# Tau-attention with a gated FFN on one core: softmax tiles turned by 64x64 products on quarters of TensorE instead of 128x128 transposes

## The chip, the core and the metric

The kernel runs on one core of one Trainium2 chip. The metric is the device time of one execution in microseconds (us). The kernel before took 859.01 us, the median of three runs (858.6 to 860.33).

## What is computed

For 8 batches, 8 heads, 576 positions and a head size of 64 the reference computes a softmax that keeps only scores within `tau` of the row's maximum, and then a feed-forward block with a convolution of three taps and a gate:

```python
scores = scale * np.matmul(q, k.transpose(0, 1, 3, 2))
thresh = np.max(scores, axis=-1, keepdims=True) - tau
scores = np.where(scores >= thresh, scores, -1000000000.0)
attn = np.exp(scores - np.max(scores, axis=-1, keepdims=True))
attn = attn / (np.sum(attn, axis=-1, keepdims=True) + 1e-09)
x = np.matmul(attn, v)          # heads side by side: 8 x 576 x 512
h = np.maximum(x @ w_in, 0.0)   # 512 -> 1024
...                             # conv_out: three taps of conv_w along the positions
gate = 1.0 / (1.0 + np.exp(-conv_out))
out = (h * gate @ w_out)        # 1024 -> 512
```

All data are float32.

## The kernel before

**Units.** Two heads make a pair, and 128 queries of a pair (or, for the last 64 queries, of two pairs) make a unit: 144 units, 18 to a batch. The function `unit` computes for each of the two heads the scores of 128 queries against 576 keys: four products of 64 by 64 weights and 288 columns, each on its own quarter of the array (line 569). VectorE takes the row maxima (line 581), ScalarE the exponential (line 588), VectorE masks and sums (line 591), and GpSimd or another engine divides by the sum (lines 627 and 629). The result is the tile `em`, with queries on the partitions.

**Turning.** The product with the values needs keys on the partitions, so `em` is turned. 70 of the 144 units go by DMA (`cross`, lines 645 to 671). The other 74 go through TensorE (`transposes`, line 673): nine blocks of 128x128, in three groups of three (`BLOCKS = 3`). A group takes one of two buffers `ps_t` of one PSUM bank, is filled by three transposes with a 128x128 identity (line 684), and ScalarE copies it to the tile `eT` (line 694; line 700 for units of two pairs). All 18 units of batch 0 are turned by TensorE.

**Attention output.** When both pairs of a half of a chunk are turned, `attend` (line 707) multiplies with the values: nine steps, each of four quarter products of 256 or 320 columns (line 720), into the same two `ps_t` buffers, one for each pair. ScalarE and VectorE read them out (lines 728 and 731).

**FFN.** A batch has two chunks of 256 and 320 positions. `mm1` (line 750) and `mm2` (line 801) are full-array products of float32r parts, three for each term; they are the largest part of TensorE's work.

**Order.** Nothing is scheduled by hand. Each step is an entry (`op`) with an engine, a cost, its inputs, its PSUM or SBUF buffers, and a rank lowered by `AHEAD`. `Plan.run` walks through these entries with its own table of costs and writes the instructions of each engine in the order that comes out; on the chip each engine then runs its list in order. For TensorE each entry has a kind: `rows` for quarter products, `turn` for transposes, `full` for the full array, and a table `SWITCH` charges a change of kind. The table charges next to nothing between `turn` and `full`.

The diff touches `transposes`, `attend`, the pool `ps_t` (line 301) and the tables of numbers at the top.

Of the kernel before, what the change touches and what calls it, by code (L numbers as in the profile page):

```python
# [10 lines left out]
F32 = mybir.dt.float32  # L11
# [5 lines left out]
AF = mybir.ActivationFunctionType  # L17
ALU = mybir.AluOpType
PSUM = bass.MemoryType.PSUM

LEAST = 2.0 ** -80
FEW = 4
AHEAD = {'mask': 5.447, 'norm': 7.929, 'parts': -2.68, 'gate': 1.222, 'evac': -0.535, 'low': 0.609, 's': 8.622, 's4': 8.87, 't': 3.177, 'a': 3.675, 'prep': 4.965, 'w': 1.618, 'load': 0.216, 'first': 3.806}

LATENCY = {'pe': 205.37, 'act': 213.173, 'dve': 118.588, 'pool': 62.545, 'ring': 1882.404}

HOLD = {'pool': 134.468, 'dve': 107.493}

NORM = (('pool', 'pool', 'pool', 'pool', 'pool', 'dve'), ('pool', 'pool', 'pool', 'act'))

# [1 line left out]
PIECES = 12  # L32
LOW = ('pool', 'pool')
HPB = 3
MOE = (3, 2)
BACKLOG = {'pool': 3000.0, 'dve': 3000.0, 'act': 9000000000.0}
WRATE = (1.713, 2.547)
ALT = 10.85

FIRST = [(0, 1), (2, 3, 4)]  # L40
GROUPS = [(0, 1), (2, 3, 4)]

EARLY = 0


SWITCH = {
# [3 lines left out]

JOINT = 0

BLOCKS = 3

FAR = 4
VB = 4
# [5 lines left out]
PTB = 1  # L62
QB = 2
CROSS = ((1, 1, 1, 1), (1, 1, 1, 1), (1, 1))
LATE = {'load': 1319.0, 'copy': 4674.0, 'rows': 335.0, 'turn': -88.0}

KEEP = {'rows': 3.322, 'cols': 0.012, 'turn': 0.252, 'full': 0.371}


class Buf:  # L70
# [17 lines left out]
class Plan:  # L88
# [13 lines left out]
    def op(self, engine, ns, fn, w=(), r=(), ahead=0.0, other=None, kind=None, late=0.0, port=False, ring=0.0):  # L102

        i = len(self.ops)
        before = set()
        for x in r:
            before.update(self.wrote[x])
            self.read.setdefault(x, set()).add(i)  # L110
        for x in w:
            before.update(self.wrote.get(x, ()))
            before.update(self.read.pop(x, ()))
            self.wrote[x] = (i,)
        before.discard(i)
# [139 lines left out]
def tile_tau_attention_gated_ffn(  # L255
# [13 lines left out]
    nc = tc.nc  # L269
    P = 128  # L270
    B, NP, _, _, S = qd.shape
    D = 64
# [11 lines left out]
    for b in range(B):  # L284
        for tiles in FIRST if not b else GROUPS:
# [4 lines left out]
                b=b, tiles=tiles, new=(o, end - o), cols=(a0, end - a0), tokens=(k0, (end if end == S else end - 1) - k0),  # L290
# [7 lines left out]
    sm = ctx.enter_context(tc.tile_pool(name="sm", bufs=4))  # L298
    far = ctx.enter_context(tc.tile_pool(name="far", bufs=FAR, space=bass.MemoryType.DRAM))
    ps_s = ctx.enter_context(tc.tile_pool(name="ps_s", bufs=2, space=PSUM))  # L300
    ps_t = ctx.enter_context(tc.tile_pool(name="ps_t", bufs=2, space=PSUM))
    ps_w = ctx.enter_context(tc.tile_pool(name="ps_w", bufs=2, space=PSUM))
    plan = Plan()
    op = plan.op
# [4 lines left out]
    ident = const("ident", [P, P], F32)  # L309
# [8 lines left out]
    for x in fews:  # L318
# [3 lines left out]
            w=[(x, "tau")], r=[(x, 0), (tau_sb, 0)], ahead=8.0  # L322
# [9 lines left out]
    gate = const("gate", [P, 1], F32)  # L332
# [32 lines left out]
    def split(src, n, name, high, low, hr, lr, lead="load"):  # L365
# [16 lines left out]
        lo, hi, a = (stage, 0), (stage, 1), (value, 0)  # L382
        w = AHEAD["w"]

# [99 lines left out]
    ring = [const(f"g{i}", [P, NFB, RING], F32R) for i in "hl"]  # L484
# [188 lines left out]
    def transposes(u, em, dsts):  # L673

        def group(b0, n):

            pt = plan.buf(ps_t, "ps_t", 2, [P, 512], F32, f"ps_t_{u}_{b0}")

            def turns():
                for i in range(n):
                    block = em[:, (b0 + i) * P:(b0 + i + 1) * P]
                    nc.tensor.transpose(out=pt[:, i * P:(i + 1) * P], in_=block, identity=ident[:])  # L684

            op("pe", n * P * 0.852, turns, w=[(pt, 0)], r=[(em, 0), (em, 1), (ident, 0)], ahead=AHEAD["t"], kind="turn")

            def source():
                return pt[:, :n * P].rearrange("p (b g n) -> p g b n", b=n, g=2)

            if dsts[0][0] is dsts[1][0]:
                (eT, g), _ = dsts
                op(
                    "act", act(n * P, True), lambda: nc.scalar.activation(eT[:, g:g + 2, b0:b0 + n, :], source(), AF.Copy),  # L694
                    w=[(eT, (g, b0))], r=[(pt, 0)], ahead=AHEAD["t"] + AHEAD["evac"]
                )
            else:
                for j, (eT, g) in enumerate(dsts):
                    op(
                        "act", act(n * D, True), lambda j=j, eT=eT, g=g: nc.scalar.activation(eT[:, g, b0:b0 + n, :], source()[:, j], AF.Copy),  # L700
                        w=[(eT, (g, b0))], r=[(pt, 0)], ahead=AHEAD["t"] + AHEAD["evac"]
                    )

        for b0 in range(0, NBLK, BLOCKS):
            group(b0, min(BLOCKS, NBLK - b0))

    def attend(of, w, parts):

        pas = [plan.buf(ps_t, "ps_t", 2, [P, 512], F32, f"pa_{i}") for i, *_ in of]
        a = AHEAD["a"]  # L710
        read = parts + [(y[3], 0) for y in of]

        for step in range(NBLK):
            def mm(step=step):
                for (_, p, eT, vt, *_), pa in zip(of, pas):
                    for h in range(2):
                        j, on = h ^ p % 2, slice(h * D, (h + 1) * D)
                        nc.tensor.matmul(  # L720
                            pa[j * D:(j + 1) * D, :w], lhsT=vt[on, step, :], rhs=eT[on, :w // D, step, :],
                            start=(step == 0), stop=(step == NBLK - 1)
                        )

            op("pe", w * 4 / 2.4 + 6, mm, w=[(pa, 0) for pa in pas], r=read, ahead=a, kind="rows")
        for (i, p, eT, vt, x, off), pa in zip(of, pas):
            def high(pa=pa, x=x, off=off):
                nc.scalar.activation(x[:, 0, off:off + w], pa[:, :w], AF.Copy)

            def low(pa=pa, x=x, off=off):  # L730
                nc.vector.tensor_tensor(x[:, 1, off:off + w], pa[:, :w], x[:, 0, off:off + w].bitcast(F32), op=ALU.subtract)

            op("act", act(w, True), high, w=[(x, 0)], r=[(pa, 0)], ahead=a + AHEAD["low"])
            op("dve", dve(w), low, w=[(x, 1)], r=[(pa, 0), (x, 0)], ahead=a + AHEAD["low"])


    def mm1(c, f, xs):
# [118 lines left out]
    for now in range(len(units) + 1):  # L856
        plan.rank = float(now)
        if now < len(units):
            i, t, n = units[now]
            c, p = pairs[i]  # L860
            (o, w), (a0, an) = chunks[c].new, chunks[c].cols
            at = TILES[t][0] - o
# [16 lines left out]
            em = unit(now, sides, n is None)  # L879
# [8 lines left out]
            if ends or alone and units[now + 1][0] != i:  # L888
                waiting = []
                for x in [i // 2 * 2, i // 2 * 2 + 1] if not alone else [i]:  # L890
# [3 lines left out]
                    off = o - a0  # L894
                    if off:
# [3 lines left out]
                            w=[(y, 2)], r=[(z, 0), (z, 1)]  # L899
# [66 lines left out]
```

## Time and profile before

| | |
|---|---|
| time, median of three runs | 859.01 us |
| time of the profiled execution | 857.31 us |
| its span, first to last instruction | 855.2 us |
| TensorE busy | 830.0 us (97%) |
| VectorE, ScalarE, GpSimd busy | 84%, 77%, 48% |
| transposes (line 684) | 666, busy 102.5 us |
| granted TensorE clock | 1.0 throughout |

The trace shows a float32 product as two products and two weight loads, so a group of four quarter products of line 569 is eight records of `PE` and eight of `PEld`. A transpose and a product of line 750 or 801 is one of each. Products are pipelined: their records overlap, and the distance from one start to the next tells the price.

### The profile page before, as it was taken

How to read it: one execution, taken by the hardware profiler on the slowest of the kernel's cores; microseconds unless marked ns; L12 is line 12 of the kernel's file. 1: busy time of each engine (PE TensorE's matmuls, PEld its weight loads, DVE VectorE, ACT ScalarE, POOL GpSimd, SP SyncE). 2: the span in 40 equal slices, each digit the busy share in tenths (PEclk: the TensorE clock that was granted, in tenths of full speed). 3: DMA queues.
4: the chain of work that ended last, by engine and by line, in shares of the span. 5: the costliest groups of instructions: out<-in, count | busy, mean ns of one | idle time of the engine just before them, and what ended most of it. 6: DMA issues, size and time to landing. Idle time of an engine off the chain costs nothing.

```text
span 855.2 us, 20928 instructions
## 1 busy us (share of the span) xinstructions
PE 830.0 (97%) x7710; PEld 609.3 (71%) x7710; DVE 719.6 (84%) x1869; ACT 656.7 (77%) x1300; POOL 410.9 (48%) x549
## 2 busy tenths in 40 slices
PE   6888999999999999999999999999999999999998
PEld 2545667767777677867778677876778677776896
DVE  6999889989979699987979879996979879997542
ACT  5999888877879678887868778886878768886542
POOL 3556544644536345553536535473545535564321
PEclk9999999999999999999999999999999999999999
DMA  7555246679666777578655676688664687555300
GB/s 260 164 164 161 75 110 185 176 206 206 164 149 179 199 196 186 134 217 234 164 149 142 204 195 164 144 211 230 162 180 127 176 215 185 139 135 143 90 26 37
DMA packets 213381, 140.72 MB, mean 165 GB/s; under 512 B 170400, under 2 KB 189088, under 8 KB 213280
## 3 DMA queue, kind: packets, MB, share of 16 engines
q1 hardware_dynamic: 212848, 139.09, 60.9%
q8 instruction: 61, 1.00, 0.5%
q10 hardware_dynamic: 432, 0.30, 0.1%
q14 instruction: 40, 0.33, 0.1%
HBM read 47.34 MB, written 50.72 MB: 115 GB/s over the span
## 4 chain that ended last, share of the span: by engine, by line
PE 86%; ACT 7%; DVE 4%; DMA 1%; issue 1%; POOL 0%; SPq 0%; DVEq 0%; ACTq 0%
PE ph L750 24%; PE po L801 23%; PE ps_s L569 17%; PE pa L720 15%; PE ps_t L684 8%; ACT em L588 2%; ACT eT L694 1%; DVE em L591 1%; DVE few L581 1%; DMA stage<-in_w_in_dram 1%; ACT stage_f L389 1%; PE pw_stage L415 0%; ACT stage L393 0%; ACT em L627 0%; DMA q<-in_qd_dram 0%
## 5 line engine op out<-in xcount | busy, mean ns | idle before, releaser
L629 POOL TENSOR_SCALAR em<-em,few 128x576 f32<-128x576 f32 x217 | 172.8, 804 | 199.1 <-DVE few L615 175.6
L581 DVE TENSOR_REDUCE few<-ps_s 128x1 f32<-128x576 f32 x288 | 209.3, 748 | 62.5 <-PE ps_s L569 60.2
L588 ACT ACTIVATE em<-ps_s,few 128x576 f32<-128x576 f32 x288 | 207.6, 745 | 56.9 <-DVE few L581 56.1
L750 PE MATMUL ph<-x,w1h 128*128 128x322 f32 (+1 forms) x1024 | 237.3, 308 | 0.0
L591 DVE SCALAR_TENSOR_TENSOR em<-ps_s,few,em 128x576 f32<-128x576 f32 x288 | 224.8, 812 | 12.9 <-ACT em L588 5.6
L344 POOL TENSOR_TENSOR gl<-t,gh 128x255 fp32r<-128x255 f32 (+9 forms) x192 | 122.9, 648 | 176.7 <-ACT gh L780 170.8
L750 PEld LDWEIGHTS ph<-x,w1h 128*128 128x128 f32 x1024 | 172.7, 189 | 20.7 <-issue 13.4
L569 PE MATMUL ps_s<-k,q 64*64 64x288 f32 x2048 | 164.4, 423 | 10.9 <-DVE em L591 5.5
L720 PE MATMUL pa<-eT,v 64*64 64x256 f32 (+1 forms) x2304 | 153.8, 404 | 0.0
L750 PE MATMUL ph<-x,w1l 128*128 128x322 f32 (+1 forms) x512 | 151.3, 295 | 0.0
L720 PEld LDWEIGHTS pa<-eT,v 64*64 64x64 f32 x2304 | 91.4, 133 | 49.2 <-issue 1.5
L801 PE MATMUL po<-w2h,gh 128*128 128x512 f32 x288 | 119.8, 416 | 0.0
L694 ACT ACTIVATE eT<-ps_t 128x384 f32<-128x384 f32 x216 | 102.3, 505 | 19.7 <-PE ps_t L684 18.8
L569 PEld LDWEIGHTS ps_s<-k,q 64*64 64x64 f32 x2048 | 67.0, 134 | 68.0 <-issue 24.7
L801 PE MATMUL po<-w2h,gl 128*128 128x512 f32 x288 | 112.9, 392 | 0.0
L801 PE MATMUL po<-w2l,gh 128*128 128x512 f32 x288 | 112.7, 391 | 0.0
L684 PE MATMUL ps_t<-ident,em 128*128 128x128 f32 x666 | 102.5, 280 | 8.8 <-ACT eT L694 5.6
L684 PEld LDWEIGHTS ps_t<-ident,em 128*128 128x128 f32 x666 | 76.0, 141 | 42.9 <-ACT eT L694 14.7
L765 DVE SCALAR_TENSOR_TENSOR t<-hp,cr 128x321 f32<-128x321 f32 (+1 forms) x128 | 78.5, 614 | 22.2 <-ACT hp L759 21.3
L750 PEld LDWEIGHTS ph<-x,w1l 128*128 128x128 f32 x512 | 96.8, 189 | 0.2
L339 POOL COPY parts<-em 128x1152 uint16<-128x1152 uint16 x70 | 82.6, 1180 | 17.2 <-POOL em L629 4.8
L772 ACT ACTIVATE t<-t,cm 128x321 f32<-128x321 f32 (+1 forms) x128 | 68.6, 538 | 27.3 <-DVE t L765 21.1
(73 smaller groups left out, 936.6 us busy)
## 6 DMA issues: line engine op xcount, KB each, us to landing
rows<-parts SPq DMA_DIRECT2D x70, 576.0 KB, 3.5
q<-in_qd_dram SPq DMA_DIRECT2D x63, 256.0 KB, 3.3
v<-in_vc_dram SPq DMA_DIRECT2D x36, 288.0 KB, 4.2
out_dram<-ot SPq DMA_DIRECT2D x36, 256.0 KB, 2.9
k<-in_kp_dram SPq DMA_DIRECT2D x31, 288.0 KB, 3.8
stage<-in_w_in_dram SPq DMA_DIRECT2D x8, 512.0 KB, 4.8
stage<-in_w_out_dram SPq DMA_DIRECT2D x8, 512.0 KB, 3.9
eT<-rows SPq DMA_TRANSPOSE x140, 4.2
```

The costliest lines, as they stand in the source:

```text
L339: engines[e].tensor_copy(dst, src)
L344: engines[e].tensor_tensor(dst, x, y, op=ALU.subtract)
L569: nc.tensor.matmul(ps[g * D:(g + 1) * D, AT + c * CH:AT + (c + 1) * CH], lhsT=q(on, h), rhs=k[on, h * CH:(h + 1) * CH], start=True, stop=True)
L581: nc.vector.tensor_reduce(few[:, nm], scores(), op=ALU.max, axis=mybir.AxisListType.XY, negate=True)
L588: nc.scalar.activation(view(), scores(), AF.Exp, bias=few[:, nm])
L591: nc.vector.scalar_tensor_tensor(view(), scores(), few[:, th], view(), op0=ALU.is_ge, op1=ALU.mult, accum_out=few[:, total])
L629: engines[e].tensor_scalar(sl, sl, LEAST, few[:, 10 + h:11 + h], op0=ALU.add, op1=ALU.mult)
L684: nc.tensor.transpose(out=pt[:, i * P:(i + 1) * P], in_=block, identity=ident[:])
L694: "act", act(n * P, True), lambda: nc.scalar.activation(eT[:, g:g + 2, b0:b0 + n, :], source(), AF.Copy),
L720: nc.tensor.matmul(pa[j * D:(j + 1) * D, :w], lhsT=vt[on, step, :], rhs=eT[on, :w // D, step, :], start=(step == 0), stop=(step == NBLK - 1))
L750: nc.tensor.matmul(ph[:, :an], lhsT=w1[w][:, cb, fs], rhs=xs[cb][:, h, :an], start=(cb == 0 and i == 0), stop=(cb == NCB - 1 and i == 2))
L801: nc.tensor.matmul(po[:], lhsT=x[:, f, at:at + P], rhs=w[:, f, :], start=(f == 0 and i == 0), stop=(f == NFB - 1 and i == 2))
```

## The change

In `transposes` a block of 128x128 is no longer turned in one transpose. Four plain float32 products, each with a 64x64 part of `em` as weights and a 64x64 part of the identity as the moving operand, turn it on the four quarters of the array. The rows of the upper and the lower half go to separate PSUM banks, so a buffer has two banks, and there is one buffer where there were two of one bank. A bank holds five blocks at most (`BLOCKS = 5`), so nine blocks go in groups of five and four, and ScalarE reads out 148 times for the 74 units in place of 222 groups. `attend` takes the same buffer, with a bank for each pair, as one piece. Turning now has the kind `rows`.

All the tables that set the order have other values (a line of them is shown), `MOE` swaps how `mm1` and `mm2` alternate, and `EARLY = 1` puts the `mm2` work of the first chunk ahead by one chunk.

```diff
-AHEAD = {'mask': 5.447, 'norm': 7.929, ... 't': 3.177, 'a': 3.675, ...}
+AHEAD = {'mask': 0.536, 'norm': 8.333, ... 't': 4.212, 'a': 3.072, ...}
-MOE = (3, 2)
+MOE = (2, 3)
-EARLY = 0
+EARLY = 1
-BLOCKS = 3
+BLOCKS = 5
+TURN = 110.0
-    ps_t = ctx.enter_context(tc.tile_pool(name="ps_t", bufs=2, space=PSUM))
+    ps_t = ctx.enter_context(tc.tile_pool(name="ps_t", bufs=1, space=PSUM))
...
-            pt = plan.buf(ps_t, "ps_t", 2, [P, 512], F32, f"ps_t_{u}_{b0}")
+            pt = plan.buf(ps_t, "ps_t", 1, [P, 2, 512], F32, f"ps_t_{u}_{b0}")
             def turns():
                 for i in range(n):
-                    block = em[:, (b0 + i) * P:(b0 + i + 1) * P]
-                    nc.tensor.transpose(out=pt[:, i * P:(i + 1) * P], in_=block, identity=ident[:])
-            op("pe", n * P * 0.852, turns, w=[(pt, 0)], r=[(em, 0), (em, 1), (ident, 0)], ahead=AHEAD["t"], kind="turn")
+                    for g in range(2):
+                        on = slice(g * D, (g + 1) * D)
+                        for j in range(2):
+                            at = (b0 + i) * P + j * D
+                            nc.tensor.matmul(
+                                pt[j * D:(j + 1) * D, g, i * D:(i + 1) * D], lhsT=em[on, at:at + D], rhs=ident[on, on],
+                                start=True, stop=True
+                            )
+            op("pe", n * TURN + 10, turns, w=[(pt, 0)], r=[(em, 0), (em, 1), (ident, 0)], ahead=AHEAD["t"], kind="rows")
             def source():
-                return pt[:, :n * P].rearrange("p (b g n) -> p g b n", b=n, g=2)
+                return pt[:, :, :n * D].rearrange("p g (b n) -> p g b n", n=D)
...
-        pas = [plan.buf(ps_t, "ps_t", 2, [P, 512], F32, f"pa_{i}") for i, *_ in of]
+        pt = plan.buf(ps_t, "ps_t", 1, [P, 2, 512], F32, f"pa_{of[0][0]}")
+        pas = [(lambda on, n=n: pt[on, n, :w]) for n in range(len(of))]
```

Two places show how the order moves. The first is TensorE in the seventh batch, where unit 122 is turned (`ps_t_122`; `po` is `mm2`, `ph` is `mm1`, `ps_s` are scores, and the number after the name of a unit's group is its first block). Before:

```order
L684 MATMUL ps_t_122_0_8974<-ident_99,em_122_8786 128x128 x3
L801 MATMUL po_26_8960<-w2h_766,gh_1146 128x512
L801 MATMUL po_26_8960<-w2h_766,gl_1181 128x512
L801 MATMUL po_26_8960<-w2l_813,gh_1146 128x512
L684 MATMUL ps_t_122_3_8988<-ident_99,em_122_8786 128x128 x3
L684 MATMUL ps_t_122_6_8992<-ident_99,em_122_8786 128x128 x3
```

And now:

```order
L810 MATMUL po_26_10551<-w2l_1047,gh_1469 128x512
L689 MATMUL ps_t_122_0_10599<-ident_99,em_122_10335 64x64 x20
L571 MATMUL ps_s_127_0_10624<-k_56_9009,q_56_10327 64x288 x4
L571 MATMUL ps_s_127_1_10631<-k_56_9009,q_56_10327 64x288 x4
L759 MATMUL ph_12_0_10639<-x_48_9803,w1h_298 128x256
L759 MATMUL ph_12_0_10639<-x_48_9803,w1l_367 128x256
L759 MATMUL ph_12_0_10639<-x_48_9803,w1h_298 128x256
L689 MATMUL ps_t_122_5_10646<-ident_99,em_122_10335 64x64 x16
L759 MATMUL ph_12_0_10639<-x_49_9808,w1h_298 128x256
```

Before, the groups of unit 122 stand between full-array products and touch no quarter product. Now each group is itself quarter work: the first shares its visit with the scores of unit 127, the second stands alone between products of `mm1`.

The second place is ScalarE, where unit 65 is read out (`eT<-ps_t`; `em<-ps_s` is the exponential, `gh` and `t` belong to the gate, `parts` to the turning by DMA). Before:

```order
L694 ACTIVATE eT_29_4796<-ps_t_65_0_4786 128x2x192
L588 ACTIVATE em_67_4804<-ps_s_67_0_4765,few3_87 128x9x64
L588 ACTIVATE em_67_4804<-ps_s_67_1_4779,few3_87 128x9x64
L780 ACTIVATE gh_1146<-t_5_5_4724 128x129
L780 ACTIVATE gh_1146<-t_5_5_4724 128x192
L337 ACTIVATE parts_66_4819<-em_66_4711 128x1152
L772 ACTIVATE t_5_6_4775<-t_5_6_4775,cm_577 128x321
L694 ACTIVATE eT_29_4796<-ps_t_65_3_4791 128x2x192
L694 ACTIVATE eT_29_4796<-ps_t_65_6_4807 128x2x192
```

And now:

```order
L702 ACTIVATE eT_29_5727<-ps_t_65_0_5802 128x2x320
L629 ACTIVATE em_67_5692<-em_67_5692,few3_87 128x9x64
L590 ACTIVATE em_68_5832<-ps_s_68_1_5794,few0_77 128x9x64
L781 ACTIVATE t_5_7_5837<-t_5_7_5837,cm_642 128x321
L339 ACTIVATE parts_67_5851<-em_67_5692 128x1152
L789 ACTIVATE gh_1469<-t_5_7_5837 128x129
L789 ACTIVATE gh_1469<-t_5_7_5837 128x192
L590 ACTIVATE em_69_5903<-ps_s_69_0_5864,few1_83 128x9x64
L702 ACTIVATE eT_29_5727<-ps_t_65_5_5882 128x2x256
```

Three readings of 384 elements a partition have become two of 640 and 512.

More of the change, by code (lines that the diff above doesn't have):

```diff
@@ L22 @@
 FEW = 4
-AHEAD = {'mask': 5.447, 'norm': 7.929, 'parts': -2.68, 'gate': 1.222, 'evac': -0.535, 'low': 0.609, 's': 8.622, 's4': 8.87, 't': 3.177, 'a': 3.675, 'prep': 4.965, 'w': 1.618, 'load': 0.216, 'first': 3.806}
-LATENCY = {'pe': 205.37, 'act': 213.173, 'dve': 118.588, 'pool': 62.545, 'ring': 1882.404}
-HOLD = {'pool': 134.468, 'dve': 107.493}
+AHEAD = {'mask': 0.536, 'norm': 8.333, 'parts': -2.514, 'gate': 1.343, 'evac': 1.378, 'low': 0.932, 's': 8.729, 's4': 8.608, 't': 4.212, 'a': 3.072, 'prep': 4.235, 'w': 2.203, 'load': 0.26, 'first': 4.822}
+LATENCY = {'pe': 189.128, 'act': 211.145, 'dve': 120.916, 'pool': 41.891, 'ring': 1550.868}
+HOLD = {'pool': 133.953, 'dve': 45.87}
 NORM = (('pool', 'pool', 'pool', 'pool', 'pool', 'dve'), ('pool', 'pool', 'pool', 'act'))
@@ L34 @@
 HPB = 3
-MOE = (3, 2)
-BACKLOG = {'pool': 3000.0, 'dve': 3000.0, 'act': 9000000000.0}
+MOE = (2, 3)
+BACKLOG = {'pool': 6860.0, 'dve': 3000.0, 'act': 9000000000.0}
 WRATE = (1.713, 2.547)
-ALT = 10.85
+ALT = 7.12
 FIRST = [(0, 1), (2, 3, 4)]
 GROUPS = [(0, 1), (2, 3, 4)]
-EARLY = 0
+EARLY = 1
 SWITCH = {
@@ L64 @@
 CROSS = ((1, 1, 1, 1), (1, 1, 1, 1), (1, 1))
-LATE = {'load': 1319.0, 'copy': 4674.0, 'rows': 335.0, 'turn': -88.0}
-KEEP = {'rows': 3.322, 'cols': 0.012, 'turn': 0.252, 'full': 0.371}
+LATE = {'load': 1775.0, 'copy': 6300.0, 'rows': 792.0, 'turn': -471.0}
+KEEP = {'rows': 3.245, 'cols': 0.008, 'turn': 0.262, 'full': 0.112}
 class Buf:
@@ L720, in mm @@
                         nc.tensor.matmul(
-                            pa[j * D:(j + 1) * D, :w], lhsT=vt[on, step, :], rhs=eT[on, :w // D, step, :],
+                            pa(slice(j * D, (j + 1) * D)), lhsT=vt[on, step, :], rhs=eT[on, :w // D, step, :],
                             start=(step == 0), stop=(step == NBLK - 1)
                         )
-            op("pe", w * 4 / 2.4 + 6, mm, w=[(pa, 0) for pa in pas], r=read, ahead=a, kind="rows")
+            op("pe", w * 4 / 2.4 + 6, mm, w=[(pt, 0)], r=read, ahead=a, kind="rows")
         for (i, p, eT, vt, x, off), pa in zip(of, pas):
             def high(pa=pa, x=x, off=off):
-                nc.scalar.activation(x[:, 0, off:off + w], pa[:, :w], AF.Copy)
+                nc.scalar.activation(x[:, 0, off:off + w], pa(slice(0, P)), AF.Copy)
             def low(pa=pa, x=x, off=off):
-                nc.vector.tensor_tensor(x[:, 1, off:off + w], pa[:, :w], x[:, 0, off:off + w].bitcast(F32), op=ALU.subtract)
-            op("act", act(w, True), high, w=[(x, 0)], r=[(pa, 0)], ahead=a + AHEAD["low"])
-            op("dve", dve(w), low, w=[(x, 1)], r=[(pa, 0), (x, 0)], ahead=a + AHEAD["low"])
+                nc.vector.tensor_tensor(x[:, 1, off:off + w], pa(slice(0, P)), x[:, 0, off:off + w].bitcast(F32), op=ALU.subtract)
+            op("act", act(w, True), high, w=[(x, 0)], r=[(pt, 0)], ahead=a + AHEAD["low"])
+            op("dve", dve(w), low, w=[(x, 1)], r=[(pt, 0), (x, 0)], ahead=a + AHEAD["low"])
     def mm1(c, f, xs):
```

## The prediction

> **What bounds the kernel now.** I read the page's head and its chain first, then the engines by stretches of the span, then TensorE's waits.
>
> ```profile
> span 855.2 us, 20928 instructions
> PE 830.0 (97%) x7710; PEld 609.3 (71%) x7710; DVE 719.6 (84%) x1869; ACT 656.7 (77%) x1300; POOL 410.9 (48%) x549
> PE 86%; ACT 7%; DVE 4%; DMA 1%; issue 1%; POOL 0%; SPq 0%; DVEq 0%; ACTq 0%
> ```
>
> TensorE is busy for 97% of the span and carries 86% of the chain that ended last. The stretches show that this isn't one regime but two (columns: the stretch, its length, then busy time of PE, PEld, DVE, ACT and POOL):
>
> ```profile
> 0.00:20.00 20.00, 11.48 (x83) 5.36 (x83) 13.16 (x37) 11.32 (x21) 5.69 (x22) 1.00 0.75 254
> 20.00:80.00 60.00, 50.62 (x466) 28.90 (x462) 56.62 (x158) 57.63 (x114) 32.71 (x38) 1.00 0.56 179
> 80.00:100.00 20.00, 19.02 (x202) 14.39 (x202) 17.56 (x41) 17.72 (x42) 14.21 (x13) 1.00 0.26 77
> 100.00:300.00 200.00, 198.99 (x1886) 144.28 (x1879) 175.71 (x455) 159.95 (x314) 96.93 (x130) 1.00 0.68 170
> 300.00:500.00 200.00, 199.86 (x1916) 148.82 (x1915) 173.23 (x460) 157.01 (x308) 97.69 (x130) 1.00 0.68 182
> 500.00:700.00 200.00, 199.35 (x1905) 147.63 (x1898) 173.92 (x457) 154.42 (x301) 97.68 (x131) 1.00 0.68 179
> 700.00:800.00 100.00, 99.11 (x950) 75.94 (x951) 86.72 (x227) 76.83 (x155) 50.42 (x67) 1.00 0.60 158
> ```
>
> From 100 to 800 us TensorE is idle for only 2.7 us of 700 (1.01 + 0.14 + 0.65 + 0.89). There, whatever TensorE gets to do beyond today's work lengthens the kernel one for one, and whatever the other engines save is worth nothing. In the first 100 us TensorE is idle for 18.9 us; from 20 to 80 us ScalarE is busy 57.63 us of 60 and VectorE 56.62, so this opening is theirs. The waits of TensorE after 100 us agree (engine, line, whom it waited for: us in total, times, longest):
>
> ```profile
> PE ps_s L569 <- DVE em L591: 2.1, 3, 0.9
> PE ps_t L684 <- ACT eT L694: 0.3, 1, 0.3
> ```
>
> So the question is what the change adds to or takes from TensorE's own stream: the price of a block, and the price of changing between quarters and the full array.
>
> **What a change of mode costs.** A stretch of the timeline near 416 us has every kind of change (start, length, engine, line, tile, count):
>
> ```profile
> 415.80 0.28 PE L750 MATMUL ph<-x,w1l 128*128 128x256 f32 x1
> 415.92 0.28 PE L750 MATMUL ph<-x,w1h 128*128 128x256 f32 x1
> 416.04 0.82 PE L684 MATMUL ps_t<-ident,em 128*128 128x128 f32 x6
> 416.61 0.36 PE L750 MATMUL ph<-x,w1h 128*128 128x256 f32 x1
> 416.81 0.28 PE L750 MATMUL ph<-x,w1l 128*128 128x256 f32 x1
> ...
> 418.19 0.28 PE L750 MATMUL ph<-x,w1l 128*128 128x256 f32 x1
> 418.31 0.28 PE L750 MATMUL ph<-x,w1h 128*128 128x256 f32 x1
> 418.51 1.20 PE L569 MATMUL ps_s<-k,q 64*64 64x288 f32 x16
> 419.65 0.87 PE L684 MATMUL ps_t<-ident,em 128*128 128x128 f32 x6
> ```
>
> A full-array product of 256 columns starts 0.12 us after the one before it. The first transpose follows at the same 0.12, and the way back is free as well: six transposes last 0.82 us, the last alone 0.27 (the median of the row below), so it began at 416.59; the second full product behind it starts at 416.81, 0.22 later, which is one transpose (0.11) and one product (0.12). Transposes among full products cost no change.
>
> ```profile
> L684 PE MATMUL ps_t<-ident,em x666: 269/273/476, 12.3 to 793.8; 128*128 128x128 f32 x167
> 428.73 1.15 PE L569 MATMUL ps_s<-k,q 64*64 64x288 f32 x16
> 419.29 0.42 PE L569 MATMUL ps_s<-k,q 64*64 64x288 f32 x4
> 402.00 0.72 PE L569 MATMUL ps_s<-k,q 64*64 64x288 f32 x8
> 402.65 0.39 PE L750 MATMUL ph<-x,w1h 128*128 128x256 f32 x1
> 402.87 0.28 PE L750 MATMUL ph<-x,w1l 128*128 128x256 f32 x1
> 402.99 0.40 PE L750 MATMUL ph<-x,w1h 128*128 128x256 f32 x2
> ```
>
> Into the quarters: scores start 0.20 after the last full product instead of 0.12, and sixteen of them last 1.20 us behind a full product against 1.15 behind other quarter products (at 428.73), because the first weight load isn't hidden. That is 0.08 to 0.09 and 0.05: 0.14 us. Out of them to the full array: four quarters run side by side as one set, a set alone lasts 0.42, and in a run of four sets the next starts (1.15 - 0.42)/3 = 0.243 us later. The second set of the eight at 402.00 began at 402.72 - 0.42 = 402.30, so a third would have come at 402.54; the full product came at 402.65, 0.11 late, and the one after it took 0.22 instead of 0.12. Together 0.21 us. Out to a transpose: the last set began at 419.29, the next was due at 419.53, the transpose came at 419.65, and six of them took 0.87 instead of 0.82: 0.16 us.
>
> **How often.** Counting in TensorE's order of instructions: before, it leaves the quarters 87 times for a full product and 49 times for a transpose, and enters them 135 times (31 of these from a transpose, which no row here prices apart; I take 0.14 too). After, it leaves them 150 times, always for a full product, and enters them 149 times. Leaving: 150 x 0.21 - 87 x 0.21 - 49 x 0.16 = 31.5 - 18.3 - 7.8 = +5.4 us. Entering: 14 x 0.14 = +2.0 us. Up to the scores of batch 1 it leaves them 18 times against 21 before, so the surplus lies wholly in the steady part. Changes that were free, transposes next to full products, are what paid for nothing before; their absence saves nothing.
>
> **What a block costs.** Before: (0.82 - 0.273)/5 = 0.109 us for a transpose. After, a block is two sets of four quarter products of 64 columns. No such product is in the trace. The nearest rows are the scores, 0.243 us for 288 columns, and the products with the values:
>
> ```profile
> 425.27 3.63 PE L720 MATMUL pa<-eT,v 64*64 64x256 f32 x64
> 428.51 0.40 PE L720 MATMUL pa<-eT,v 64*64 64x256 f32 x4
> 419.05 0.15 PEld L569 LDWEIGHTS ps_s<-k,q 64*64 64x64 f32 x4
> ```
>
> Sixteen sets in 3.63 us, less the last one's 0.40, are 0.215 us for 256 columns. Both give 0.84 ns a column, so 64 columns give 0.054 us a set and 0.108 a block. The weights of the next set are loaded meanwhile; a load that isn't hidden showed as 0.05, so load and stream are about equally long and neither should hold up the other much. I take 0.111: 666 x 0.002 = +1.3 us. The lower bound is 0.108 (-0.7 us), for a column takes no less in any row. The upper one is the spacing per product that a long run shows: 3.63/64 = 0.057 us, eight to a block, 0.45 us, or +229 us; below the rivals say why it isn't my value.
>
> Products of different quarters do start closer than that: four of them, each 0.402 long at the least (row below), are over in 0.42 us at 419.29, so they start within 0.02 us, and four weight loads lie within 0.15.
>
> ```profile
> L569 PE MATMUL ps_s<-k,q x2048: 402/403/740, 4.1 to 779.4; 64*64 64x288 f32 x187
> ```
>  The Trainium skill, "TensorE: Matmul & The Clock Gate" (Wait — 56ns, not 53.3ns?), says that the distance between starts never falls below about 25 ns, however few columns a product has. By that, eight products would make a block of at least 0.20 us and the sum about +61 us instead of +1.3. The four starts within 0.02 us speak against it for products of different quarters, in short bursts; no row shows them kept up.
>
> **ScalarE and the single buffer.** Reading out has these neighbours:
>
> ```profile
> L694 ACT ACTIVATE eT<-ps_t 128x384 f32<-128x384 f32 x216 | 102.3, 505 | 19.7 <-PE ps_t L684 18.8 <-ACT t L772 0.7
> L808 ACT ACTIVATE ot<-po 128x512 f32<-128x512 f32 x36 | 21.3, 596 | 31.7 <-PE po L801 31.4
> L728 ACT ACTIVATE x<-pa 128x320 fp32r<-128x320 f32 x32 | 12.1, 433 | 7.0 <-PE pa L720 6.9
> 416.56 0.49 ACT L694 ACTIVATE eT<-ps_t 128x384 f32<-128x384 f32 x1 [0.45 <-PE ps_t L684]
> ```
>
> From 320 to 512 elements it takes 0.163 us more, 0.85 ns each, so 640 cost about 0.70 us. A unit takes 0.60 + 0.70 = 1.30 us against 3 x 0.505 = 1.52: 0.2 us saved, 15 us over 74 units, of which the steady part keeps nothing. In the opening ScalarE is full; 14 units are turned before the scores of batch 1, so at most 3 us. I take -2 us, bounds 0 and -3.
>
> The second group of a unit must now wait until the first is read out. ScalarE began 0.52 us after the first of three transposes at 416.04, so 0.30 after the last; with 0.70 of reading and a hand-back of some 0.05 that is 1.05 us from the last start. In the order, 30 of the 116 groups that follow a group have no more between them than two scores' sets (four sets, 0.97 us), and lack up to 0.1 us each; the others have more. I take +1 us; bounds 0, and 10 if ScalarE comes 0.3 late at each of those 30. Behind a late group wait the scores and FFN products in TensorE's list, and so VectorE's maxima. `attend` held both buffers before as well, and its read-out has at least 2 us of other products behind it: nothing. The `mm2` work of chunk 0 that `EARLY` moves is the same work and lies in mid-kernel, covered by TensorE's own full list; at the end the list still closes with the last chunk. Nothing, and DMA on SP has the same 354 issues in both orders.
>
> **Sum.** 5.4 + 2.0 + 1.3 + 1.0 - 2.0 = +7.7 us on the profiled execution of 857.3 us (span 855.2): 865.0. The median of the runs, 859.0, lies 1.7 above that execution, so I expect 866.7 us. A measurement of this kernel can tell about 0.2%, 1.7 us, from no change.
>
> **Rivals.**
> - *The opening gives it back (not slower).* 14.8 us of TensorE's 18.9 idle us in the first 100 lie after its first product at about 4.1 us (those before it can't be had), and 2.7 us later on. Without my -2, the sum is 868.7; if the new order and ScalarE's relief win back half to all of the 17.5 us, the time is 851 to 860. It decides from 9.7 us: there the kernel is back at 859. For it: ScalarE is the fullest engine there and is what the change relieves. Against it: the relief is 3 us, VectorE has the same 56.62 of 60 us to do, and less than the full amount is only a draw. I give 0.18, of which 0.13 faster and 0.05 within 0.2%.
> - *A block costs about twice as much.* If load and stream of a quarter don't overlap when both are 0.05 us, a block is 2 x (0.054 + 0.05) = 0.21 us: 666 x 0.10 = +67 us, 932 us; if starts are what holds, it sets in where a product takes more than 0.111/8 = 0.014 us to issue, and by the long run's 0.057 it would be 1094 us. For it: 16 instructions in 0.11 us is denser than any long run here, where 64 products took 3.63 us. Against it: those bursts, and the loads that start with the set before them. 0.08.
> - *The one buffer makes TensorE wait.* ScalarE is 78% busy in order (157.01 of 200 us); if it came 0.1 us late at each of 148 groups, that would be 15 us in place of 1: 881 us. For it: no second buffer takes up a delay any more. Against it: before, the same hand-over cost 0.3 us after the opening. 0.08.
>
> The forecast itself gets 0.66 (862 to 874 us), of which 0.03 ends within 0.2%. So faster 0.13, the same 0.08, slower 0.79. The range 857 to 882 us leaves out the twofold block and the better part of the first rival, and takes in the third and both ends of the read-out term.
>
> **What would show it.** In the new profile, twenty turning products (40 records) in a row should take 0.56 us from the first start to the next product's, at 64 columns; transposes' 666 records give way to 5328 of the new form. The first product behind the quarters should still come 0.11 late and take 0.10 more, 150 times. TensorE's idle time after 100 us should stay below 5 us, and the opening should end some 2 us sooner at most. I am wrong if a block takes under 0.105 or over 0.13 us, if the first 100 us hold more than 6 us more of TensorE's work, or if waits for the read-out exceed 5 us.

## The result and the profile after

| | before | after |
|---|---|---|
| median | 859.03 us (4 runs, 858.6 to 860.33) | 868.94 us (4 runs, 868.16 to 870.91) |
| profiled execution, its span | 857.31, 855.2 us | 870.91, 869.1 us |
| mean granted TensorE clock in it | 1.0 | 0.996 |

The changed kernel takes 1.0125 times as long (95% interval 1.0109 to 1.0141): 9.9 us more by the medians. The profiled execution of after is the slowest of its four, the profiled one of before lay below its median, so the two traces stand 13.9 us apart by their spans; some 4 us of that lie between single executions and medians, and the text comes back to them. The head of the page and its chain:

```profile
span 869.1 us, 30149 instructions
PE 844.7 (97%) x12372; PEld 639.9 (74%) x12372; DVE 725.8 (84%) x1869; ACT 656.4 (76%) x1223; POOL 417.0 (48%) x550
PE 88%; ACT 5%; DVE 4%; issue 1%; DMA 1%; SPq 1%; POOL 0%; ACTq 0%; DVEq 0%
```

TensorE carries 88% of the chain and is 14.7 us busier; VectorE is 6.2 us busier with the same 1869 instructions, ScalarE's busy time is what it was. By stretches (stretch, length, busy time of PE, PEld, DVE, ACT, POOL, then the granted clock):

```profile
0.00:20.00 20.00, 11.23 (x209) 7.20 (x209) 13.19 (x38) 11.39 (x19) 5.74 (x21) 1.00 0.77 244
20.00:80.00 60.00, 51.62 (x1005) 27.96 (x1001) 52.07 (x145) 53.37 (x97) 30.59 (x35) 0.94 0.52 171
80.00:100.00 20.00, 18.88 (x319) 13.93 (x319) 18.38 (x44) 18.26 (x36) 14.01 (x13) 1.00 0.20 61
100.00:300.00 200.00, 198.59 (x3065) 148.03 (x3055) 177.63 (x461) 157.34 (x290) 101.04 (x132) 1.00 0.70 170
300.00:500.00 200.00, 199.43 (x2902) 154.17 (x2901) 173.70 (x452) 155.89 (x287) 98.81 (x130) 1.00 0.73 178
500.00:700.00 200.00, 199.88 (x2908) 156.59 (x2910) 175.30 (x457) 154.62 (x286) 99.63 (x131) 1.00 0.72 177
700.00:800.00 100.00, 99.64 (x1448) 75.78 (x1437) 89.01 (x227) 75.50 (x141) 49.13 (x65) 1.00 0.62 159
```

From 100 to 800 us TensorE is again idle for only 2.5 us (1.41 + 0.57 + 0.12 + 0.36), as little as before. There the extra time is work and changes of mode, not waiting; TensorE's waits of that part say the same (engine, line, whom it waited for: us in total, times, longest):

```profile
PE pa L729 <- ACT eT L708: 0.8, 1, 0.8
PE ps_t L689 <- ACT eT L702: 0.5, 1, 0.5
PE ph L759 <- ACT hp L768: 0.4, 1, 0.4
```

TensorE waits 0.5 us for the single buffer here. In the opening ScalarE and VectorE have less to do (53.37 and 52.07 us from 20 to 80 us, where before had 57.63 and 56.62), and the granted clock stands at 0.94, where before had 1.00. Two short stretches hold all of the lost clock:

```profile
43.40:46.80 3.40, 2.98 (x52) 1.76 (x55) 2.56 (x8) 1.78 (x4) 1.45 (x2) 0.50 0.00 0
74.10:77.50 3.40, 3.40 (x24) 1.22 (x20) 2.60 (x6) 2.63 (x5) 1.38 (x2) 0.50 0.05 16
```

**The new product.** Two turning groups in the timeline (start, length, engine, line, tile, count), the first alone between full products, the second ahead of scores:

```profile
226.28 0.28 PE L759 MATMUL ph<-x,w1l 128*128 128x256 f32 x1
226.39 0.28 PE L759 MATMUL ph<-x,w1h 128*128 128x256 f32 x1
226.60 0.81 PE L689 MATMUL ps_t<-ident,em 64*64 64x64 f32 x40
227.34 0.50 PE L810 MATMUL po<-w2h,gh 128*128 128x512 f32 x1
227.68 0.39 PE L810 MATMUL po<-w2h,gl 128*128 128x512 f32 x1
227.91 0.39 PE L810 MATMUL po<-w2l,gh 128*128 128x512 f32 x1
...
306.71 0.69 PE L689 MATMUL ps_t<-ident,em 64*64 64x64 f32 x32
307.23 0.67 PE L571 MATMUL ps_s<-k,q 64*64 64x288 f32 x8
```

And the row of the tile (shortest, median, longest):

```profile
L689 PE MATMUL ps_t<-ident,em x5328: 213/218/366, 11.5 to 812.2; 64*64 64x64 f32 x198
```

Eight sets of four behind a full product take 307.23 - 306.71 = 0.52 to the next quarter product; less the 0.05 for the first weight load that isn't hidden, 0.47/8 = 0.059 us a set. The ten sets at 226.60 agree: 0.81, less the last set's 0.24 (0.218 and the 0.02 within a set) and 0.05, over nine steps is 0.058. Over eight inner steps of each group of ten in the trace, the median of a step is 0.0584. A block of two sets thus costs 0.117 us, not 0.111.

The changes of mode cost what they cost before. The turning starts 0.21 after a product that is otherwise followed at 0.12 (0.09, and 0.05 for the load); the full product comes at 227.34, 0.74 after the first start, where 0.05 + 10 x 0.0584 = 0.63 are the sets: 0.11 late, and the one behind it takes 0.34 instead of 0.23: 0.22 in all.

The readings of ScalarE (elements, count, busy time and mean ns):

```profile
L702 ACT ACTIVATE eT<-ps_t 128x640 f32<-128x640 f32 x72 | 50.6, 702 | 7.5 <-PE ps_t L689 7.4
L702 ACT ACTIVATE eT<-ps_t 128x512 f32<-128x512 f32 x72 | 43.1, 599 | 23.4 <-PE ps_t L689 22.8
```

They take 0.702 and 0.599 us, to the hundredth what was estimated.

**The bill.** TensorE's order, priced with distances from start to start, splits the span from the first score to the last product. "Work" is every product at its distance (a transpose 0.109, a turning block 0.117); "changes" are the changes of mode in the order at the mean distances of these traces (0.216 out to a full product, 0.167 out to a transpose, 0.142 in); "rest" is what is left: waiting, and time at half clock. The opening runs from the first score to the first score of unit 36, the first of batch 2.

| us | opening: work, changes, rest | later: work, changes, rest | sum |
|---|---|---|---|
| before | 147.4, 14.3, 25.2 | 619.5, 32.4, 8.2 | 847.0 |
| after | 147.0, 14.3, 29.6 | 625.1, 39.2, 5.6 | 860.8 |

The whole order has 6.9 us more of changes of mode (before rounding), 5.2 us more of work (666 x 0.0078), and 1.8 us more of rest: 4.4 more in the opening, 2.6 less later. (2.0 us of the later work is `mm2` that stood ahead of unit 36 before.)

### The profile page after: what moved, and what is told of

It is laid out like the page before. It is cut to its first block, busy times and chain, and to the rows that moved or that the text cites. A ratio compares the mean times of both kernels' runs of the same rounds, so it can differ in the third digit from the quotient of the medians.

```text
span 869.1 us, 30149 instructions
## 1 busy us (share of the span) xinstructions
PE 844.7 (97%) x12372; PEld 639.9 (74%) x12372; DVE 725.8 (84%) x1869; ACT 656.4 (76%) x1223; POOL 417.0 (48%) x550
## 4 chain that ended last, share of the span: by engine, by line
PE 88%; ACT 5%; DVE 4%; issue 1%; DMA 1%; SPq 1%; POOL 0%; ACTq 0%; DVEq 0%
PE ph L759 23%; PE po L810 23%; PE ps_s L571 16%; PE pa L729 16%; PE ps_t L689 9%; DVE em L593 1%; ACT em L590 1%; ACT eT L702 1%; DVE few L583 1%; DMA rows<-parts 1%; PE pw_stage L417 1%; SPq L671 1%; DVE t L774 0%; ACT stage_f L391 0%; ACT em L629 0%
## 5 line engine op out<-in xcount | busy, mean ns | idle before, releaser
L631 POOL TENSOR_SCALAR em<-em,few 128x576 f32<-128x576 f32 x218 | 175.5, 812 | 200.4 <-DVE few L617 145.1
L590 ACT ACTIVATE em<-ps_s,few 128x576 f32<-128x576 f32 x288 | 206.7, 741 | 51.7 <-DVE few L583 49.4
L759 PE MATMUL ph<-x,w1h 128*128 128x322 f32 (+1 forms) x1024 | 229.0, 304 | 0.4 <-ACT hp L768 0.4
L346 POOL TENSOR_TENSOR gl<-t,gh 128x255 fp32r<-128x255 f32 (+9 forms) x192 | 125.9, 666 | 169.3 <-ACT gh L789 165.0
L759 PEld LDWEIGHTS ph<-x,w1h 128*128 128x128 f32 x1024 | 170.1, 189 | 20.2 <-issue 8.6
L689 PEld LDWEIGHTS ps_t<-ident,em 64*64 64x64 f32 x5328 | 100.1, 136 | 47.6 <-ACT eT L702 15.6
L729 PEld LDWEIGHTS pa<-eT,v 64*64 64x64 f32 x2304 | 96.0, 133 | 46.7 <-ACT eT L702 1.9
L689 PE MATMUL ps_t<-ident,em 64*64 64x64 f32 x5328 | 111.0, 223 | 9.8 <-ACT eT L702 7.0
L702 ACT ACTIVATE eT<-ps_t 128x640 f32<-128x640 f32 (+1 forms) x144 | 93.7, 650 | 30.9 <-PE ps_t L689 30.2
L339 ACT ACTIVATE parts<-em 128x1152 uint16<-128x1152 uint16 x70 | 81.6, 1166 | 7.7 <-POOL em L631 5.7
```

Of the source, the lines that this page charges most:

```text
L346: engines[e].tensor_tensor(dst, x, y, op=ALU.subtract)
L590: nc.scalar.activation(view(), scores(), AF.Exp, bias=few[:, nm])
L631: engines[e].tensor_scalar(sl, sl, LEAST, few[:, 10 + h:11 + h], op0=ALU.add, op1=ALU.mult)
L689: nc.tensor.matmul(pt[j * D:(j + 1) * D, g, i * D:(i + 1) * D], lhsT=em[on, at:at + D], rhs=ident[on, on], start=True, stop=True)
L729: nc.tensor.matmul(pa(slice(j * D, (j + 1) * D)), lhsT=vt[on, step, :], rhs=eT[on, :w // D, step, :], start=(step == 0), stop=(step == NBL ...
L759: nc.tensor.matmul(ph[:, :an], lhsT=w1[w][:, cb, fs], rhs=xs[cb][:, h, :an], start=(cb == 0 and i == 0), stop=(cb == NCB - 1 and i == 2))
```

## The experiments

"Before" was timed again with them: medians 858.71 (with the first four), 858.65 (with the next four) and 857.89 us (with the last three).

**The same order with transposes.** After's order, groups and buffer, but each block is one transpose:

```diff
-                    for g in range(2):
...
+                    nc.tensor.transpose(out=pt[:, i // 4, i % 4 * P:(i % 4 + 1) * P], in_=block, identity=ident[:])
```

> The changed kernel with its order, its groups of five and four and its single buffer untouched, instruction for instruction, but each block is turned by one 128x128 transpose again. Theory (changes of mode and the price of a block): counted in this order, it leaves the quarters 63 times to a full product (0.216 us) and 81 times to a transpose (0.167), enters them 143 times (0.142 to 0.145), and passes 150 times between transposes and full products for nothing; that is 48.0 us of changes against 53.6, and 666 blocks cost 0.109 instead of the 0.117 that the new profile shows, 5.2 us less. Together 10.8 us less than the changed kernel: 858 us. Rival one (the new order is at fault, whatever turns the blocks): it stays at 868 to 869 us. Rival two (the single buffer makes TensorE wait): it stays above 865 us, and waits for the read-out of more than 5 us show after the opening.

861.99 us, 1.0034 of before (1.0022 to 1.0046). The quarter products themselves are 7 us of the 9.9, at the same order of steps. By the bill they are 10.9 (5.2 of work, 53.6 - 47.9 = 5.7 of changes); 2 to 4 us of that do not show, because TensorE, now quicker, waits more (rest 37.3 instead of 35.2). Its waits for the one buffer after 100 us:

```profile
PE ps_t L686 <- ACT eT L696: 2.4, 9, 0.6
```

Nine waits in place of one: what the transposes save is partly waited away. So the change of the product is the larger part of the loss, and the order with one buffer is by itself no gain (3.3 us above before).

**New code with the old numbers, and the old code with the new ones.** The first is after with all the numbers of before (`AHEAD`, `LATENCY`, `HOLD`, `MOE`, `BACKLOG`, `ALT`, `EARLY`, `LATE`, `KEEP`):

```diff
-AHEAD = {'mask': 0.536, 'norm': 8.333, ... 't': 4.212, 'a': 3.072, ...}
+AHEAD = {'mask': 5.447, 'norm': 7.929, ... 't': 3.177, 'a': 3.675, ...}
...
-MOE = (2, 3)
+MOE = (3, 2)
-EARLY = 1
+EARLY = 0
```

> The changed code with every number of the order as before (AHEAD, LATENCY, HOLD, MOE, BACKLOG, ALT, EARLY, LATE, KEEP). Theory: its order leaves the quarters 169 times and enters them 168 times, 60.4 us of changes against 53.6 with the new numbers, so about 6.8 us more than the changed kernel: 876 us. Rival one (the new numbers cost the time): it comes back towards 859 us. Rival two (single buffer): waits for the read-out grow, since these numbers were not made for one buffer, and it exceeds 880 us.

The second is the same diff turned round, on before:

> The kernel before, transposes in three groups through two buffers, with the new numbers for the order. Theory: 50.5 us of changes of mode against 46.7, so about 4 us more than before: 863 us. Rival one (the new numbers cost the time): 868 us or more.

902.22 us, 1.0508 (1.0486 to 1.0531), and 873.28 us, 1.0166 (1.0148 to 1.0183). Both cost more than expected. The new numbers are worth 33 us to the new code and cost the old code 14.6: they are fitted to one program, and no gain of their own shows. Of the first kernel's 43.5 us over before, about half lies in the opening: unit 36 comes 208.7 us after the first score instead of 186.9, though TensorE's work there is the same 147.0. Its stretches:

```profile
20.00:80.00 60.00, 48.06 (x897) 26.24 (x893) 55.01 (x145) 51.08 (x93) 29.44 (x34) 0.97 0.45 148
80.00:100.00 20.00, 16.11 (x305) 12.04 (x301) 16.91 (x33) 17.28 (x32) 11.88 (x10) 0.99 0.29 94
100.00:300.00 200.00, 194.15 (x2998) 141.95 (x2991) 172.50 (x437) 151.88 (x283) 97.71 (x126) 0.98 0.60 155
```

TensorE is idle far longer than in after (16.11 busy of 20 against 18.88, then 194.15 of 200 against 198.59): here it does wait, and from 100 us on too. Behind unit 36 the old numbers also make for more changes of mode (45.0 us against 39.2) and more rest (12.9 against 5.6).

**The buffer and the groups alone.** Transposes again, still planned as `turn`, in groups of five and four through one buffer of two banks, which `attend` takes as one piece as in after, with the old numbers:

```diff
+BLOCKS = 5
-    ps_t = ctx.enter_context(tc.tile_pool(name="ps_t", bufs=2, space=PSUM))
+    ps_t = ctx.enter_context(tc.tile_pool(name="ps_t", bufs=1, space=PSUM))
-            pt = plan.buf(ps_t, "ps_t", 2, [P, 512], F32, f"ps_t_{u}_{b0}")
+            pt = plan.buf(ps_t, "ps_t", 1, [P, 2, 512], F32, f"ps_t_{u}_{b0}")
```

> The kernel before with its numbers and its transposes, but groups of five and four through one buffer of two banks. Theory: 50.1 us of changes of mode against 46.7 (three groups to a unit leave more freedom than two), a little wait for the buffer, and 2 us back in the opening from ScalarE: 861 to 863 us. Rival two (the single buffer is what costs): 866 us or more. A third view, that fewer read-outs by ScalarE help by themselves: below 858 us.

880.91 us, 1.025 (1.0225 to 1.0275): 22 us, the rival's side and more. Its opening takes 205.5 us (work 145.3, changes 13.2, rest 47.0 where before has 25.2), and after unit 36 it is only 6.3 us behind before. So this buffer with its groups does hurt where the engines wait for one another. How much of it is the one buffer and how much the groups of five and four was not separated, and numbers that were fitted to other code can cost as much by themselves (14.6 us above, with both buffers in place).

```profile
20.00:80.00 60.00, 47.67 (x406) 23.70 (x405) 49.94 (x138) 49.65 (x90) 29.27 (x34) 0.92 0.44 139
80.00:100.00 20.00, 17.24 (x127) 12.54 (x125) 15.35 (x35) 16.78 (x31) 10.54 (x9) 0.91 0.33 110
100.00:300.00 200.00, 193.61 (x1843) 140.28 (x1844) 174.78 (x453) 158.26 (x296) 100.92 (x132) 0.98 0.59 159
300.00:500.00 200.00, 199.09 (x1892) 145.48 (x1890) 172.16 (x452) 154.47 (x285) 96.26 (x127) 1.00 0.69 177
```

TensorE idles more, the clock falls to half in stretches of 3.4 or 6.8 us (20.5 us in the opening, the last over before 109 us), and later, from 300 us on, it is full again. TensorE's own waits of the first 200 us name the masking, on which the scores' buffers wait, more than the read-out:

```profile
PE ps_s L571 <- DVE em L593: 9.9, 7, 2.2
PE ps_t L686 <- ACT eT L696: 6.5, 9, 1.7
PE ps_s L571 <- issue: 3.4, 1, 3.4
```

Before has there:

```profile
PE ps_s L569 <- DVE em L591: 6.2, 6, 2.2
PE ps_t L684 <- ACT eT L694: 5.6, 10, 1.4
```

All of TensorE's waits in these 200 us come to 30.0 us, in before to 19.1. These 10.9 us and some 10 us lost to half clock make up nearly all of the 21.8 us more of rest. The direct wait for the read-out is only 0.9 us of it; the masks are 3.7 and one wait without a releaser 3.4. That these come late because of the buffer is argued, not shown. With the new numbers little of this is left; after's waits in the first 100 us:

```profile
PE ps_t L689 <- ACT eT L702: 6.4, 9, 1.4
PE ps_s L571 <- DVE k L343: 4.0, 1, 4.0
PE ps_s L571 <- DVE em L593: 3.9, 5, 2.2
```

**Which of the numbers.** The new code with the old numbers, but the new `AHEAD`:

```diff
-AHEAD = {'mask': 5.447, 'norm': 7.929, ... 't': 3.177, 'a': 3.675, ...}
+AHEAD = {'mask': 0.536, 'norm': 8.333, ... 't': 4.212, 'a': 3.072, ...}
```

> The changed code with the old numbers, except AHEAD (how far ahead of its turn each step is ranked), which is the new one. The changed code took 902 us with all old numbers and 869 with all new ones; 7 us of these 33 are changes of mode by count, the rest are waits. If AHEAD is what fits the order to one buffer: most of it comes back, 872 to 880 us (by count 5 us of mode changes remain). If not: it stays above 890 us.

With the old numbers and only `EARLY` new:

```diff
-EARLY = 0
+EARLY = 1
```

> The changed code with the old numbers, except EARLY = 1. If the place of the first chunk's second product is what fits the order to one buffer: below 890 us. If it is worth nothing, as I priced it: 902 us, plus 0.7 us of mode changes by count.

And after itself without it:

```diff
-EARLY = 1
+EARLY = 0
```

> The changed kernel with EARLY = 0, all other new numbers kept: the second product of the first chunk goes back to its old place. By the order, changes of mode cost 0.7 us more (152 exits, 151 entries). If moving this work is worth nothing, as I priced it: 869 to 870 us. If it is what keeps the opening short with one buffer (the rival): the opening grows towards the 209 us that it takes with all the old numbers, and the time passes 880 us.

882.55 us (1.0293, 1.0278 to 1.0309), 905.68 (1.0563, 1.0544 to 1.0583) and 869.68 (1.0139, 1.0124 to 1.0154). `AHEAD` alone brings back 20 of the 33 us, 13.6 of them in the opening (195.1 instead of 208.7 us), a little less than the 22 us or more that were expected. `EARLY` is worth nothing in after: the intervals of 869.68 and of after's 868.94 overlap. With the old numbers it costs 3.5 us more instead of helping.

**How the set's price depends on its columns.** The moving operand gets 96 columns of the identity instead of 64, the last 32 of them written over by the next block; the lower half of each tile then holds other values.

```diff
-                                pt[j * D:(j + 1) * D, g, i * D:(i + 1) * D], lhsT=em[on, at:at + D], rhs=ident[on, on],
+                                pt[j * D:(j + 1) * D, g, i * D:i * D + 96], lhsT=em[on, at:at + D], rhs=ident[on, :96],
```

> The changed kernel, each turning product moving 96 columns of the identity instead of 64 (the further 32 are overwritten by the next block or left unread; the lower half of each tile gets other values, so the output is not the reference's). Theory (the 0.058 us a set is the weight load, which a longer stream hides): the stream rules, 96 x 0.84 ns + 2 ns = 0.082 to 0.083 us a set, 1332 sets, +33 us: 902 us. Rival (each set has a fixed cost of 0.005 us above its stream, whatever its length): 0.085 to 0.086 us a set and +37 us: 906 us. The spacing of sets in the trace tells them apart better than the time.

One run, 892.1 us. A group in its timeline, and the product behind it:

```profile
461.27 1.06 PE L689 MATMUL ps_t<-ident,em 64*64 64x96 f32 x40
462.25 0.42 PE L759 MATMUL ph<-x,w1h 128*128 128x322 f32 x1
```

The median product lasts 0.243 us, so (1.06 - 0.26 - 0.05)/9 = 0.083 us a set; 96 columns at 0.84 ns are 0.081. Then each turning product in two halves of 32 columns, with the same result:

```diff
+                            for half in range(0, D, 32):
...
+                                    pt[j * D:(j + 1) * D, g, i * D + half:i * D + half + 32], lhsT=em[on, at:at + D],
+                                    rhs=ident[on, g * D + half:g * D + half + 32], start=True, stop=True
```

> The changed kernel with each turning product split into two of 32 columns, so twice as many weight loads and products for the same result. Theory (the weight load of 64 columns holds up each set): the spacing of sets stays at 0.056 to 0.058 us though the stream is halved, a block costs 0.23 us, and 1332 more sets make +77 us: about 946 us. Rival one (stream plus a fixed 0.005 us): 0.032 us a set, +8 us: 877 us. Rival two (starts of products are what is slow, 25 ns each as a floor): 0.1 us a set, +190 us or more.

One run, 959.76 us:

```profile
505.00 1.37 PE L690 MATMUL ps_t<-ident,em 64*64 64x32 f32 x80
506.30 0.42 PE L760 MATMUL ph<-x,w1h 128*128 128x322 f32 x1
```

Twenty sets: (1.37 - 0.24 - 0.05)/19 = 0.057 us (0.0584 in the median over eight inner steps of each group), although 32 columns stream in 0.027. So a set has a floor of 0.058 us that fewer columns don't lower, and 96 columns come to lie above it. At 64 columns the floor binds, by 0.004 us a set over the 0.054 of the stream. What makes the floor is not shown. It isn't a price per record: in after, the four products of a set and the four loads for the next one start within 0.023 us. The load of 64 columns remains the likely cause, by its own pace: in each quarter loads follow one another at 0.058 us with 64 columns and with 32 alike. But a product doesn't wait that long for its load: with 32 columns it begins 0.028 us after the load does, with 64 columns 0.056. No kernel with a shorter load was run. Whole times were off both ways: 23 us in place of 33 for the first (its opening hides part), more than expected for the second, whose opening stretched.

**Quarter products only where they change no mode.** After's order, but of its 148 groups only the 20 that stand between quarter work on both sides use the quarter products; the others are transposes.

```diff
+                if (u, b0) in STAY:
+...
+                else:
+                    nc.tensor.transpose(out=pt[:, i // 4, i % 4 * P:(i % 4 + 1) * P], in_=block, identity=ident[:])
```

> The changed kernel in its own order, instruction for instruction, but a group is turned by quarter products only where quarter work stands on both sides of it (20 of 148 groups, 17 of them in batches 0 and 1); the other 128 groups are turned by 128x128 transposes. Theory: counted in the order, changes of mode cost 42.7 us against 48.0 with transposes alone and 53.6 in the changed kernel, and nearly all blocks 0.109 again: up to 4.6 us less than with transposes alone where TensorE is the bound, but most of these groups lie in the opening, where it isn't. So 858 to 861.5 us. Rival (the order of the changed kernel is at fault): no better than the 862.0 of transposes alone.

858.66 us (10 runs) against 858.65 (13 runs): 1.0000 (0.9991 to 1.0010). Two rows show the mix (products, busy time and mean ns, then idle time ahead of them):

```profile
L699 PE MATMUL ps_t<-ident,em 128*128 128x128 f32 x576 | 88.3, 280 | 5.3 <-ACT eT L711 4.7 <-POOL em L633 0.4
L692 PE MATMUL ps_t<-ident,em 64*64 64x64 f32 x720 | 16.6, 234 | 4.9 <-ACT eT L711 3.5 <-POOL em L633 1.1
```

Its changes of mode are 42.7 us by the count, 4.0 under before and 10.9 under after; its work 767.6 (before 766.9, after 772.1). So the quarter product is worth having only beside quarter work. That it merely equals before lies in the rest: 38.4 us against 33.4, 3.9 more in the opening (where its trace has one stretch at half clock, 1.7 us) and 1.1 more behind it. The other two kernels in this order have more of it than before, too (after 35.2, the same order with transposes 37.3), but not every kernel with the one buffer: priced the same way, after without `EARLY` has about as much as before, and the one with 96 columns some 10 us less.

**Does the opening wait for TensorE, or TensorE for the opening?** After, with the first of the two products that leave a weight's residue (`rest`, with the identity) done twice: 12 more products of 512 columns, all in the opening.

```diff
+                nc.tensor.matmul(pw[:, :n], lhsT=ident[:], rhs=v(), start=True, stop=True)
                 nc.tensor.matmul(pw[:, :n], lhsT=ident[:], rhs=v(), start=True, stop=False)
```

> The changed kernel with the first product that forms the low part of a weight piece done twice (12 more products of 512 columns, some 0.5 us each, all in the first 80 us). Theory (the opening's loss comes from stretches of 3.4 us at half clock that follow TensorE's idleness there): with TensorE busier the half-clock stretches become fewer, and the time falls by 1 to 3 us although there is more work. Rival (TensorE's work in the opening is on the path): up to 6 us more, 875 us. If both cancel, or the stretches stay: 868 to 870 us, and the granted clock tells which.

872.02 us, 1.0153 (1.0136 to 1.0169), 3 us over after, unit 36 1.8 us later.

```profile
20.00:80.00 60.00, 54.14 (x971) 29.46 (x975) 50.44 (x141) 52.36 (x93) 30.95 (x35) 1.00 0.49 163
```

TensorE does 2.5 us more than after in this stretch, at a clock of 1.00 (all four runs had a mean of 0.999 or 1.0). With more work the half-clock stretches are gone, and the kernel is slower all the same. TensorE's work in the opening is thus partly on the path, though it is idle for 18 of the first 100 us.

## Why the prediction was right, point by point

- **TensorE bounds the steady part one for one.** Held: 2.7 us idle became 2.5, and the additions to its stream came out as time.
- **Leaving and entering quarters, +7.4.** Held: the price of each change is the same beside the new products (0.21 to 0.22 out, 0.14 in), and by the count of the whole order they came to +6.9. Dropping the 128x128 transposes, which change no mode beside full products, is the larger part of the loss; the mixed kernel, which keeps them there, gives it back.
- **A block, 0.111 us, +1.3.** The mechanism held, the size was off: 0.117, +5.2. The step that failed is "load and stream are about equally long and neither should hold up the other much": a set takes the longer of its stream and a floor, and that is 0.058, not the 0.054 of the columns. The bound named for being wrong (over 0.13) was not reached. The lower bound, that a column takes no less in any row, holds for the quarter products and transposes alone: the full products move 256 columns in 0.12 us. Sets four wide are kept up at 0.0584 us over 40 and 32 records in a row, 0.015 us a product, so the rival with the doubled block fell. The Trainium skill, "TensorE: Matmul & The Clock Gate" (Wait — 56ns, not 53.3ns?), says that starts never come closer than about 25 ns. For products that go round four quarters the trace disagrees: 15 ns.
- **Reading out, 0.70 and 0.60.** Held to the hundredth.
- **The one buffer, +1 (0 to 10), and the opening, -2 (0 to -3).** In the steady part the buffer cost nothing that shows: the rest fell by 2.6 us. The waits for the read-out are 6.4 us in the first 100 us and 0.5 behind them. By the letter that exceeds the 5 us that the prediction named for being wrong, but before had 5.2 and 0.3 already, so the mark told nothing; they grew by 1.4. The opening failed in its sign: no gain, but 4.4 us more of rest in the profiled execution. At most 3.4 of these are the two stretches at half clock, which before has in other executions as well; TensorE's waits of the first 200 us come to 18.6 us, in before to 19.1. ScalarE was busy 3.6 us less in the first 100 us (86.67 to 83.02), but TensorE did not get its products sooner; unit 36 came 4.1 us later. The step that failed is "In the opening ScalarE is full ... I take -2 us": it took the relief of ScalarE for time in the opening and priced the buffer by the groups of the steady part alone. With the old numbers one buffer and its groups cost 22 us, most of them in the opening; with the new ones at most a few are left. The third rival was wrong for this kernel, as its waits for the read-out in the steady part (0.5 us) show. The issues on SP that the prediction counts as 354 are 411 in both traces; that they are the same held.
- **`EARLY` at nothing.** Held for this kernel.
- **The sum.** +7.7 was forecast, +9.9 measured: 6.9 of changes, 5.2 of blocks and, by the medians, -2.2 of rest, where +1 and -2 had been put. The traces have +1.8 of rest; the 4 us between come with the two executions that were traced, in part because before's had no stretch at half clock and after's had two. That the rest comes near the forecast is luck: the opening was to gain and did not, the steady part was to lose and gained. So is part of the sum: the blocks came out 3.9 us above the forecast, the changes and the rest 1.7 below it.

What stays open: what the opening's loss is beyond the half clock, and what the one buffer costs without its groups; the kernel with more work in the opening had no such stretches but added work in doing so. Of a planner that knows by place which form to take, and could save more than the mixed kernel's 4.0 us of changes, nothing was tried; no kernel here beat before.

## What to carry to other kernels

Where TensorE is full, count the changes between quarters and the whole array in the order itself and price them (here 0.21 out and 0.14 in): a cheaper or denser form of a product is a gain only if it saves more than the changes that it puts on its sides. A short product costs the longer of its stream and a floor (here 0.058 us for a set of four, likely the pace of the weight loads), so an estimate from the columns of a long one is a lower bound. Numbers that set an order belong to the code that they were fitted to, and code and order have to be compared by exchanging each alone.

## What the runs showed of the hardware that was not expected

- The granted clock falls to 0.50 for stretches of 3.4 us, or two or three times that (10.2 us in the kernel with two halves, from 49.4 us), in after only in the first 80 us; in the kernels with the old numbers it comes later, too (0.98 as the mean from 100 to 300 us), and with two halves once more at 793.5 us. The Trainium skill, "TensorE: Matmul & The Clock Gate" (What's actually happening), tells of a free-running activity window of about 3.4 us. The length agrees, and after's two stretches begin 30.7 us apart, nine times that. In the 3.4 us ahead of each, TensorE is busy for 44% and 53% of the time (the first two lines, from after). That alone doesn't bring a stretch, for before and the kernel with more work have such 3.4 us as well, and a full clock behind them (the last two lines):

```profile
40.00:43.40 3.40, 1.50 (x72) 1.23 (x72) 3.02 (x18) 3.04 (x6) 0.10 (x1) 1.00 0.73 274
70.70:74.10 3.40, 1.81 (x47) 1.06 (x48) 1.99 (x8) 2.01 (x5) 1.98 (x3) 1.00 0.65 244
45.40:48.80 3.40, 1.29 (x11) 0.82 (x9) 3.37 (x10) 3.40 (x8) 2.09 (x3) 1.00 0.03 12
41.00:44.40 3.40, 1.25 (x70) 0.97 (x64) 3.07 (x16) 3.13 (x6) 0.44 (x1) 1.00 0.62 200
```

- A stretch is not always there: of 29 timings of before beside the experiments, the nine at a mean clock of 0.996 took 859.0 to 860.4 us, the eleven at 1.0 took 857.1 to 858.4. Two stretches (each 1.7 us of lost clock, 3.4 of 857 are 0.004) cost some 1.9 us between the medians, 859.75 and 857.89.
- A quarter product in fp32 with 64-column weights has a floor of 0.058 us for a set of four (32 columns: 0.057, 64: 0.058), and a set of 96 columns, whose stream is longer, takes 0.083.
- A transpose of 128x128 stands among full products at no price, but coming from quarter products it costs 0.16 us: there it behaves as full-array work does.
